# Batch 0's k in two halves of its heads on 96 partitions, its v let go by the second half's landing, and the last row tile in two column parts

## The chip, the cores and the metric

The kernel runs on one core of one Trainium2 chip. The metric is the device time of one execution in microseconds (us). Kernels are compared by executions on the same chip, one after the other. The granted clock is TensorE's clock as a share of full speed.

## The reference

Eight batches of attention with 8 heads, 576 positions and 64 columns a head. k and v are averaged over 8 neighbouring positions first, so that there are 72 pooled positions. Then a two-layer network with a GELU (tanh form) runs over all 4608 tokens.

```python
k_p = k.reshape(B, H, Sp, pool, D).mean(axis=3)          # B=8, H=8, S=576, D=64, pool=8, Sp=72
v_p = v.reshape(B, H, Sp, pool, D).mean(axis=3)
scores = scale * np.matmul(q, k_p.transpose(0, 1, 3, 2))
attn = softmax(scores)                                    # written out in the reference
x = (attn @ v_p).transpose(0, 2, 1, 3).reshape(B * S, H * D)     # 4608 x 512
h = x @ w_in                                              # 512 x 2048
out = gelu_tanh(h) @ w_out                                # 2048 x 512
```

## The kernel before

The network takes the tokens in 9 groups of 512. While TensorE runs the network for one group, the attention of a later batch is slipped in between. Batch 0 has nothing to hide behind: its attention is the head of the kernel, some 22 us. All inputs are fp32 in device memory. k's 576 rows of 2 KB (8 positions of 64 numbers) lie 4 to a partition on 128 partitions, and the last 64 rows in a fifth column block beside the end of v:

```python
KR = 4
kts = [consts.tile([128, KR + 1, 512], F32, name=f"kt{i}") for i in range(2)]

def load_k(b, engs):
    rows = k[b].rearrange("h (j l) d -> (h j) (l d)", l=8)
    main = rows[0:128 * KR].rearrange("(p r) c -> p r c", r=KR)
    n = KR // len(engs)
    for i, eng in enumerate(engs):
        eng.dma_start(out=kts[b % 2][:, i * n:(i + 1) * n], in_=main[:, i * n:(i + 1) * n])
    engs[0].dma_start(out=kts[b % 2][64:128, KR], in_=rows[128 * KR:])
    # ... and v's rows 64 to 71 of each head, into kts[b % 2][0:64, KR]

def load_v(b, engs):                      # v's rows 0 to 63: one half of the heads on 64 partitions each
    rows = v[b].rearrange("h (j l) d -> j h (l d)", l=8)
    for i in range(2):
        engs[i % len(engs)].dma_start(out=vts[b % 2][64 * i:64 * i + 64], in_=rows[0:64, 4 * i:4 * i + 4])

load_k(0, [nc.sync, nc.scalar])           # three queues: sync's, scalar's, GpSimd's
load_v(0, [nc.sync, nc.scalar])
load_q(0, 0, 1)                           # load_q, w_in, w_out: GpSimd's queue, cast to bf16 on the way
load_q(0, 1, 2)
load_w_in(0)
load_w_in(1)
load_k(1, [nc.gpsimd])
load_q(1)
load_v(1, [nc.gpsimd])
for i in range(4):                        # w_out in quarters
    ...
```

A batch's eight values are summed by three adds on VectorE (256, 128 and 64 columns wide), pooled k is turned by TensorE, the scores go through an exponential on ScalarE, and the products with pooled v are multiplied by an inverse of the sums (`inverse0`). `spin` puts matmuls on a zero tile into TensorE's waits; what that does for its clock is measured in warm and warm_full below (in warm_full the granted clock stays at full from 20.2 us on). The end of batch 0's attention:

```python
for f in v_steps(0):
    f()
inverse0(1, 0, 6)
spin(4, 4)
av0(0, 0, 4)                              # the first attention product
mult0(0, 0, 4)
den0(0, 2, 2)
inverse0(0, 2, 2)
av0(1, 0, 0)
# ... two more products with fillers between, then the clearing for batch 1, then the first layer
```

Each row tile of 128 tokens of the second layer is 16 matmuls of 512 columns, one copy out of PSUM and four stores.

The softmax here doesn't subtract the row's maximum and nothing guards it: scores larger than these inputs give would overflow.

## Time and profile before

| | |
|---|---|
| time | 309.19 us, median of 3 (308.62 to 309.35) |
| span of the profiled execution | 306.5 us, mean granted clock 0.999 |
| first attention product, first network layer | 17.18 and 22.08 us |
| landing of v of batch 0, of the last quarter of w_out | 14.45 and 43.99 us |
| start of the last copy out, from there to the end | 302.11 and 4.38 us |

The views are read thus. The page gives each engine's busy time and the chain of work that ended last. A line of the timeline is: start, length, engine, source line, operation, output and input tiles, and in brackets the idle time in front of it and what ended that. "Landing" is the moment the last of the 16 DMA engines reports a transfer done. The lines themselves are in the prediction below.

### The profile page before, as it was taken

What the parts mean: (1) busy time and instruction counts of PE and PEld (TensorE: products, weight loads), DVE (VectorE), ACT (ScalarE), POOL (GpSimd) and SP (SyncE); (2) the same over time, 40 slices, a digit from 0 to 9 for tenths busy, and PEclk for the clock granted to TensorE, in tenths of its full rate; (3) what the DMA queues carried; (4) which work ended last, traced back from release to release, by engine and by line L of the source; (5) the groups of instructions that cost most, each with busy time, mean ns of one, the idle gap of its engine ahead of it and who ended that gap; (6) DMA issues with size and microseconds to landing.
All of it is one profiled execution on the core that took longest, in us unless ns stands there. A gap on an engine that the chain in (4) does not pass through costs nothing.

```text
span 306.5 us, 4325 instructions
## 1 busy us (share of the span) xinstructions
PE 298.2 (97%) x1518; PEld 157.4 (51%) x1548; DVE 150.4 (49%) x334; ACT 219.0 (71%) x402; POOL 36.3 (12%) x69
## 2 busy tenths in 40 slices
PE   8999999999999999999999999999999999999994
PEld 3555555555555555555555555555555555445441
DVE  5868557573677057806681559245933630110021
ACT  1686679868987798779977998789868987206400
POOL 7103002305004000220014000400000000000000
PEclk9999999999999999999999999999999999999999
DMA  7999996987957952596159725662101210121022
GB/s 225 266 257 253 214 186 137 299 176 177 269 146 167 247 122 51 114 282 156 34 112 266 168 56 106 200 151 71 35 1 36 63 41 2 34 70 34 2 70 68
DMA packets 30359, 41.12 MB, mean 134 GB/s; under 512 B 18113, under 2 KB 18113, under 8 KB 29441
## 3 DMA queue, kind: packets, MB, share of 16 engines
q0 software_dynamic: 7856, 25.43, 34.9%
q1 hardware_dynamic: 21888, 14.09, 19.2%
q10 hardware_dynamic: 592, 1.31, 1.2%
q8 instruction: 12, 0.20, 0.3%
q14 instruction: 11, 0.08, 0.1%
HBM read 36.70 MB, written 9.44 MB: 151 GB/s over the span
## 4 chain that ended last, share of the span: by engine, by line
PE 83%; DMA 12%; POOL 1%; issue 1%; ACT 0%; DVE 0%; POOLq 0%
PE PS L345 38%; PE PS L336 36%; DMA kt<-in_k_dram 7%; DMA w_out_b<-in_moe_w_out_dram 5%; PE PS L239 4%; PE PS L261 4%; PE PS L174 1%; POOL w_in_b L105 0%; POOL qb L86 0%; POOL w_out_b L113 0%; DVE osb L350 0%; ACT e L247 0%; ACT ld L269 0%; ACT ld L268 0%; POOL identb masks.py:199 0%
## 5 line engine op out<-in xcount | busy, mean ns | idle before, releaser
L345 PE MATMUL PS<-w_out_b,gT 128*128 128x512 bf16 x560 | 134.2, 379 | 0.9
L336 PE MATMUL PS<-xT,w_in_b 128*128 128x512 bf16 x563 | 126.2, 379 | 0.6
L342 ACT ACTIVATE gT<-PS 128x512 bf16<-128x512 f32 x144 | 81.1, 604 | 47.5 <-PE PS L336 47.4
L336 PEld LDWEIGHTS <-w_in_b 128*128 128x128 bf16 x576 | 64.7, 113 | 57.2
L345 PEld LDWEIGHTS <-gT 128*128 128x128 bf16 x576 | 56.1, 97 | 56.7 <-issue 1.1
L350 DVE COPY osb<-PS 128x512 f32<-128x512 f32 x36 | 24.9, 691 | 98.3 <-PE PS L345 95.3
L279 DVE TENSOR_TENSOR xT<-PS,rc 64x288 bf16<-64x288 f32 x112 | 51.0, 455 | 31.6 <-ACT rc L271 29.3
L247 ACT ACTIVATE e<-PS 72x576 bf16<-72x576 f32 (+1 forms) x64 | 41.0, 646 | 9.1 <-PE PS L239 8.2
L239 PE MATMUL PS<-qT,kT 128*72 128x288 bf16 (+1 forms) x128 | 25.9, 286 | 0.9 <-ACT qT L214 0.6
L271 ACT ACTIVATE rc<-ld 128x288 f32<-128x288 f32 x56 | 24.8, 443 | 1.8
L314 ACT ACT_TABLE_LOAD x17 | 21.8, 1283 | 4.3 <-issue 4.1
L268 ACT ACTIVATE ld<-PS 64x288 f32<-64x288 f32 x56 | 22.8, 407 | 1.3
L269 ACT ACTIVATE ld<-PS 64x288 f32<-64x288 f32 x56 | 22.5, 402 | 1.3
L261 PE MATMUL PS<-e,vp 72*128 72x288 bf16 (+1 forms) x112 | 23.1, 286 | 0.0
L139 DVE TENSOR_TENSOR kt<-kt 128x1280 f32<-128x1280 f32 (+5 forms) x18 | 18.8, 1044 | 5.5 <-DMA kt<-in_v_dram 2.6
L239 PEld LDWEIGHTS <-kT 128*72 128x72 bf16 (+1 forms) x128 | 13.2, 105 | 15.2 <-DVE qT L216 1.2
L448 POOL COPY gate<-qT 1x2 bf16<-1x2 bf16 x6 | 1.0, 174 | 140.0 <-DMA qT<-qb 140.0
L139 DVE TENSOR_TENSOR vt<-vt 128x1024 f32<-128x1024 f32 (+1 forms) x16 | 15.3, 956 | 1.8 <-DMA vt<-in_v_dram 1.5
L184 DVE COPY kT<-PS 64x288 bf16<-64x288 bf16 (+2 forms) x48 | 13.0, 319 | 6.2 <-PE PS L174 6.1
L362 PE MATMUL PS<-idle 128*128 128x512 bf16 x39 | 11.9, 447 | 1.2 <-DVE idle L127 1.2
L261 PEld LDWEIGHTS <-vp 72*128 72x128 bf16 (+1 forms) x112 | 11.0, 98 | 3.8
L81 POOL DMA_DIRECT2D vt<-in_v_dram x14 | 9.0, 655 | 7.5 <-DMA w_in_b<-in_moe_w_in_dram 5.5
(47 smaller groups left out, 90.0 us busy)
## 6 DMA issues: line engine op xcount, KB each, us to landing
out_dram<-osb SPq DMA_DIRECT2D x142, 64.0 KB
kt<-in_k_dram POOLq DMA_DIRECT2D x7, 1024.0 KB, 6.2
vt<-in_v_dram POOLq DMA_DIRECT2D x14, 512.0 KB, 8.6
qb<-in_q_dram POOLq DMA_DIRECT2D x7, 576.0 KB, 11.6
w_in_b<-in_moe_w_in_dram POOLq DMA_DIRECT2D x2, 1024.0 KB, 16.7
w_out_b<-in_moe_w_out_dram POOLq DMA_DIRECT2D x4, 512.0 KB, 13.9
kt<-in_k_dram POOLq DMA_DIRECT2D x7, 128.0 KB, 5.9
kt<-in_v_dram POOLq DMA_DIRECT2D x14, 64.0 KB, 5.7
```

Of the source, the lines that this page charges most:

```text
L139: nc.vector.tensor_tensor(out=o, in0=a, in1=b, op=ALU.add)
L239: nc.tensor.matmul(out=PS[:n, bank + e, :CH].rearrange("j (t p) -> j t p", p=32), lhsT=kTs[b % 2][c][:, h, :n], rhs=qTs[b][:, h // 4, :, h ...
L247: nc.scalar.activation(out=e[:n], in_=PS[:n, bank:bank + 2, :CH], func=ACT.Exp, scale=1.0 / 64.0)
L261: nc.tensor.matmul(out=PS[:, bank + x, :CH], lhsT=window(vps[b % 2][:n], 2 * pr + x), rhs=e[:n, x, :], start=True, stop=True)
L268: nc.scalar.activation(out=ld[0:64], in_=PS[64:128, bank, :CH], func=ACT.Ln)
L269: nc.scalar.activation(out=ld[64:128], in_=PS[0:64, bank + 1, :CH], func=ACT.Ln)
L271: nc.scalar.activation(out=rc, in_=ld, func=ACT.Exp, scale=-1.0)
L279: nc.vector.tensor_tensor(out=xT[rows, pr, col:col + CH], in0=PS[rows, bank + x, :CH], in1=rc[rows], op=ALU.mult)
L336: nc.tensor.matmul(out=PS[:, h_bank(g, fo), c0:c1], lhsT=w_in_b[fo // 8][:, ko, q * 512 + j:(q + 1) * 512:4], rhs=xT[:, ko, r0 + c0:r0 + c ...
L342: nc.scalar.activation(out=gTs[g][:, fo, :], in_=PS[:, h_bank(g, fo), :], func=ACT.Gelu_apprx_tanh)
L345: nc.tensor.matmul(out=PS[:, o_bank(g, r), :], lhsT=gTs[g][:, fo, r * 128:(r + 1) * 128], rhs=w_out_b[:, fo, :], start=(fo == 0), stop=(fo ...
L350: nc.vector.tensor_copy(out=osb, in_=PS[:, o_bank(g, r), :])
```

## The change

Its intent: the first scores need only the lower half of the heads of k and the first half of q, so only these are fetched at first. Upper k follows in GpSimd's queue, and v, which is needed last, is held back until upper k has landed, so that it doesn't compete. A half of k has 288 rows, 3 to a partition on 96 partitions. Batch 1's v goes to sync's queue, the order after v is tightened, and the last row tile is cut into 384 and 128 columns so that its last copy is short.

```diff
-    KR = 4
+    KR = 3
-    kts = [consts.tile([128, KR + 1, 512], F32, name=f"kt{i}") for i in range(2)]
+    kts = [consts.tile([128, 2 * KR, 512], F32, name=f"kt{i}") for i in range(2)]
+    K0 = (0, 32)
+    def load_k(b, i, engs):
+        rows = k[b].rearrange("(i h) (j r l) d -> i (h j) (r l d)", i=2, r=KR, l=8)[i]
+        n = 4 * KH // len(engs)
+        for x, eng in enumerate(engs):
+            eng.dma_start(out=kts[b % 2][K0[i] + x * n:K0[i] + (x + 1) * n, KR * i:KR * i + KR],
+                          in_=rows[x * n:(x + 1) * n].rearrange("p (r c) -> p r c", r=KR))
 ...
-    load_k(0, [nc.sync, nc.scalar])
-    load_v(0, [nc.sync, nc.scalar])
+    load_k(0, 0, [nc.sync, nc.scalar])
     load_q(0, 0, 1)
+    load_k(0, 1, [nc.gpsimd])
+    load_v_last(0, nc.scalar)
     load_q(0, 1, 2)
 ...
     load_w_in(0)
+    for p in (slice(32, 64), slice(64, 128)):
+        nc.gpsimd.tensor_copy(out=vts[0][p, 0, 0:1], in_=kts[0][p, KR, 0:1])
+    load_v(0, [nc.sync])
     load_w_in(1)
 ...
-    load_v(1, [nc.gpsimd])
 ...
     inverse0(1, 0, 6)
-    spin(4, 4)
-    av0(0, 0, 4)
-    mult0(0, 0, 4)
+    spin(2, 4)
     den0(0, 2, 2)
     inverse0(0, 2, 2)
+    spin(2, 4)
+    av0(0, 0, 4)
+    mult0(0, 0, 4)
+    nc.vector.memset(vts[1][:, 0, 0:1], 0.0)
+    load_v(1, [nc.sync])
 ...
+    for t in kts:
+        nc.vector.memset(t[96:128, 0:KR], 0.0)
+    nc.vector.memset(kts[1][0:32, 2 * KR - 1], 0.0)
 ...
+    for c0, c1, bank in ((0, 384, o_bank(g, 3)), (384, DM, 4)):
+        for fo in range(FO):
+            p2_mm(g, 3, fo, bank, c0, c1)
+        store(g, 3, bank, c0, c1)
```

Cut: the transposes and copies of k by halves, v's last rows as two column blocks, fewer fillers, and the arguments that the column parts need. The two GpSimd copies are the hold: they read upper k and write into v's tile, so v's load can't be issued before upper k is in (in the profile after, upper k landed at 11.05 and sync issued v at 11.40).

More of the change, by code (lines that the diff above doesn't have):

```diff
@@ L63, with load_v_last @@
     vts = [consts.tile([128, 4, 512], F32, name=f"vt{i}") for i in range(2)]
-    kts = [consts.tile([128, KR + 1, 512], F32, name=f"kt{i}") for i in range(2)]
-    def load_k(b, engs):
-        rows = k[b].rearrange("h (j l) d -> (h j) (l d)", l=8)
-        main = rows[0:128 * KR].rearrange("(p r) c -> p r c", r=KR)
-        n = KR // len(engs)
-        for i, eng in enumerate(engs):
-            eng.dma_start(out=kts[b % 2][:, i * n:(i + 1) * n], in_=main[:, i * n:(i + 1) * n])
-        engs[0].dma_start(out=kts[b % 2][64:128, KR], in_=rows[128 * KR:])
+    kts = [consts.tile([128, 2 * KR, 512], F32, name=f"kt{i}") for i in range(2)]
[6 more added lines that the diff above has]
+                          in_=rows[x * n:(x + 1) * n].rearrange("p (r c) -> p r c", r=KR))
+    def load_v_last(b, eng):
         rows = v[b].rearrange("h (j l) d -> j h (l d)", l=8)
         for i in range(2):
-            engs[-1].dma_start(out=kts[b % 2][32 * i:32 * i + 32, KR], in_=rows[64:, 4 * i:4 * i + 4])
+            eng.dma_start(out=kts[b % 2][0:32, KR + i], in_=rows[64:, 4 * i:4 * i + 4])
     def load_v(b, engs):
@@ L107, with load_k_all @@
     load_w_in(0)
+    for p in (slice(32, 64), slice(64, 128)):
+        nc.gpsimd.tensor_copy(out=vts[0][p, 0, 0:1], in_=kts[0][p, KR, 0:1])
+    load_v(0, [nc.sync])
     load_w_in(1)
-    load_k(1, [nc.gpsimd])
+    def load_k_all(b):
+        for i in range(2):
+            load_k(b, i, [nc.gpsimd])
+        load_v_last(b, nc.gpsimd)
+    load_k_all(1)
     load_q(1)
-    load_v(1, [nc.gpsimd])
     for i in range(4):
@@ L119 @@
     kTs = [[consts.tile([128, H, 128], BF16, name=f"kT{i}{e}") for e in range(2)] for i in range(2)]
-    kps = [consts.tile([128, KR + 2, D], BF16, name=f"kp{i}") for i in range(2)]
+    kps = [consts.tile([128, 2 * KR + 1, D], BF16, name=f"kp{i}") for i in range(2)]
     vps = [consts.tile([128, H, 2, D], BF16, name=f"vp{i}") for i in range(2)]
@@ L127 @@
     nc.vector.memset(idle, 0.0)
+    nc.vector.memset(kts[0][0:32, 2 * KR - 1], 0.0)
     nc.vector.memset(kTs[0][0], 0.0)
@@ L139, in add, with k_steps @@
         nc.vector.tensor_tensor(out=o, in0=a, in1=b, op=ALU.add)
-    def k_steps(b, c=slice(0, KR + 1)):
-        t = kts[b % 2]
+    def k_steps(b, i0=0, i1=2):
+        c = slice(i0 * KR, i1 * KR)
+        n = K0[i1 - 1] + 4 * KH
+        t = kts[b % 2][0:n]
         return [lambda: add(t[:, c, 0:256], t[:, c, 0:256], t[:, c, 256:512]),
                 lambda: add(t[:, c, 0:128], t[:, c, 0:128], t[:, c, 128:256]),
-                lambda: add(kps[b % 2][:, c], t[:, c, 0:64], t[:, c, 64:128])]
+                lambda: add(kps[b % 2][0:n, c], t[:, c, 0:64], t[:, c, 64:128])]
     def v_moves(b):
@@ L152, in v_moves @@
             nc.sync.dma_start(out=vps[b % 2][64 - 64 * i:72 - 64 * i, 4 * i:4 * i + 4, 0],
-                              in_=kps[b % 2][32 * i:32 * i + 32, KR])
+                              in_=kps[b % 2][0:32, KR + i])
     def v_steps(b):
@@ L168, in half_bank, with trans_k_mm @@
         return PS[:, bank, :].bitcast(BF16)
-    def trans_k_mm(b, bank, r0=0, r1=KR + 1, n=128):
-        tp = half_bank(bank)[:, 0:(KR + 1) * 128].rearrange("p (r c) -> p r c", c=128)
+    def trans_k_mm(b, i, bank):
+        tp = half_bank(bank)[:, 0:2 * KR * 128].rearrange("p (r c) -> p r c", c=128)
         kf = kps[b % 2].rearrange("p r d -> p (r d)")
-        for r in range(r0, r1):
-            nc.tensor.transpose(out=tp[:n, r, :], in_=kf[:, r * D:r * D + n], identity=identb)
-    def trans_k_copy(b, e, bank, lower=True, upper=True):
-        tp = half_bank(bank)[0:D, 0:(KR + 1) * 128].rearrange("p (r c) -> p r c", c=128)
-        o = kTs[b % 2][e][e * 64:(e + 1) * 64]
-        copy = nc.vector.tensor_copy
-        def heads(h0, h1, c0, j0, j1):
-            copy(out=o[:, h0:h1, c0:c0 + (j1 - j0) * KR].rearrange("p h (j r) -> p h j r", r=KR),
-                 in_=tp[:, 0:KR, h0 * KH:h1 * KH].rearrange("p r (h j) -> p h j r", j=KH)[:, :, j0:j1])
-        if lower:
-            heads(0, 4, 0, 0, KH)
-        if upper:
-            heads(4, H - 1, 64, 0, 16)
-            heads(4, H - 1, 0, 16, KH)
-            copy(out=o[:, H - 1, 64:72].rearrange("p (j r) -> p j r", r=KR),
-                 in_=tp[:, 0:KR, (H - 1) * KH:128].rearrange("p r j -> p j r"))
-            copy(out=o[:, H - 1, 72:128], in_=tp[:, KR, 64:120])
-            copy(out=o[:, H - 1, 0:8], in_=tp[:, KR, 120:128])
@@ new lines, in trans_k_mm, with trans_k_copy, part @@
+        n, m = (128, 128) if b else (K0[i] + 4 * KH, D)
+        for r in range(i * KR, i * KR + KR):
+            nc.tensor.transpose(out=tp[0:m, r, 0:n], in_=kf[0:n, r * D:r * D + m], identity=identb[0:n, 0:n])
+    def trans_k_copy(b, e, i, bank):
+        tp = half_bank(bank)[0:D, 0:2 * KR * 128].rearrange("p (r c) -> p r c", c=128)
+        tp = tp[:, i * KR:i * KR + KR, K0[i]:K0[i] + 4 * KH].rearrange("p r (h j) -> p h j r", j=KH)
+        o = kTs[b % 2][e][e * 64:(e + 1) * 64, 4 * i:4 * i + 4]
+        def part(c0, j0, j1, r0=0, r1=KR):
+            n = r1 - r0
+            nc.vector.tensor_copy(out=o[:, :, c0:c0 + (j1 - j0) * n].rearrange("p h (j r) -> p h j r", r=n),
+                                  in_=tp[:, :, j0:j1, r0:r1])
+        if i == 0:
+            part(0, 0, KH)
+        else:
+            part(64, 0, 21)
+            part(127, 21, 22, 0, 1)
+            part(0, 21, 22, 1, 3)
+            part(2, 22, KH)
@@ L197, in trans_k @@
     def trans_k(b, bank):
-        trans_k_mm(b, bank)
+        for i in range(2):
+            trans_k_mm(b, i, bank)
         for e in range(2):
-            trans_k_copy(b, e, bank)
+            for i in range(2):
+                trans_k_copy(b, e, i, bank)
     def trans_q_mm(b, i, t0, n, bank):
@@ L342, in gelu, with p2_mm, store @@
         nc.scalar.activation(out=gTs[g][:, fo, :], in_=PS[:, h_bank(g, fo), :], func=ACT.Gelu_apprx_tanh)
-    def p2_mm(g, r, fo):
-        nc.tensor.matmul(out=PS[:, o_bank(g, r), :], lhsT=gTs[g][:, fo, r * 128:(r + 1) * 128], rhs=w_out_b[:, fo, :],
-                         start=(fo == 0), stop=(fo == FO - 1))
-    def store(g, r):
-        osb = opool.tile([128, DM], F32, name="osb")
-        nc.vector.tensor_copy(out=osb, in_=PS[:, o_bank(g, r), :])
+    def p2_mm(g, r, fo, bank, c0=0, c1=DM):
+        nc.tensor.matmul(out=PS[:, bank, c0:c1], lhsT=gTs[g][:, fo, r * 128:(r + 1) * 128],
+                         rhs=w_out_b[:, fo, c0:c1], start=(fo == 0), stop=(fo == FO - 1))
+    osbs = {}
+    def store(g, r, bank, c0=0, c1=DM):
+        if (g, r) not in osbs:
+            osbs[g, r] = opool.tile([128, DM], F32, name="osb")
+        osb = osbs[g, r]
+        nc.vector.tensor_copy(out=osb[:, c0:c1], in_=PS[:, bank, c0:c1])
         for n in range(4):
-            b, c = divmod(g * GROUP + r * 128 + n * 32, S)
+            b, col = divmod(g * GROUP + r * 128 + n * 32, S)
             rows = out[b * S:(b + 1) * S].rearrange("(p t e) d -> e t p d", t=TP, e=2)
-            eng = nc.scalar if (g, r) == (NG - 1, 3) and n % 2 else nc.sync
-            eng.dma_start(out=rows[c // CH, c % CH // 32], in_=osb[n * 32:(n + 1) * 32, :])
+            eng = nc.scalar if c1 - c0 < DM and n % 2 else nc.sync
+            eng.dma_start(out=rows[col // CH, col % CH // 32, :, c0:c1], in_=osb[n * 32:(n + 1) * 32, c0:c1])
     def spin(n, bank):
@@ L364 @@
     act_set(EXP_SET)
-    spin(22, 1)
-    for f in k_steps(0, slice(0, KR)):
+    spin(13, 1)
+    for f in k_steps(0, 0, 1):
         f()
@@ L371, in scores @@
         expo(0, c, pr, bank)
-    trans_k_mm(0, 4, 0, KR, D)
-    trans_k_copy(0, 0, 4, upper=False)
     trans_q(0, *QG[0], 5, nc.scalar)
-    trans_q(0, *QG[1], 6, nc.vector)
-    trans_k_copy(0, 1, 4, upper=False)
+    trans_q(0, *QG[1], 6, nc.scalar)
+    spin(3, 4)
+    trans_k_mm(0, 0, 4)
+    trans_k_copy(0, 0, 0, 4)
+    trans_k_copy(0, 1, 0, 4)
     scores(0, 0, 2)
@@ L380 @@
     spin(2, 7)
-    for f in k_steps(0, slice(KR, KR + 1)):
+    for f in k_steps(0, 1, 2):
         f()
     scores(1, 0, 2)
-    trans_k_mm(0, 4, KR, KR + 1, D)
-    trans_k_copy(0, 0, 4, lower=False)
+    trans_k_mm(0, 1, 4)
+    trans_k_copy(0, 0, 1, 4)
     for h in range(H):
@@ L389 @@
         nc.tensor.matmul(out=PS[64 - 64 * i:72 - 64 * i, 7, h * D:(h + 1) * D],
-                         lhsT=identb[0:64, 32 * i + h % 4:32 * i + 32:4], rhs=kps[0][0:64, KR],
+                         lhsT=identb[0:32, h % 4:32:4], rhs=kps[0][0:32, KR + i],
                          start=True, stop=True)
@@ L400 @@
     trans_q(0, *QG[3], 6, nc.vector)
-    trans_k_copy(0, 1, 4, lower=False)
+    trans_k_copy(0, 1, 1, 4)
     spin(3, 7)
@@ L410 @@
     inverse0(1, 0, 6)
-    spin(4, 4)
+    spin(2, 4)
+    den0(0, 2, 2)
+    inverse0(0, 2, 2)
+    spin(2, 4)
     av0(0, 0, 4)
     mult0(0, 0, 4)
-    den0(0, 2, 2)
-    inverse0(0, 2, 2)
+    nc.vector.memset(vts[1][:, 0, 0:1], 0.0)
+    load_v(1, [nc.sync])
+    den0(1, 2, 6)
+    inverse0(1, 2, 6)
     av0(1, 0, 0)
     mult0(1, 0, 0)
-    spin(3, 6)
-    den0(1, 2, 6)
-    inverse0(1, 2, 6)
-    spin(3, 4)
     av0(0, 2, 4)
     mult0(0, 2, 4)
-    spin(3, 0)
+    spin(2, 0)
     av0(1, 2, 0)
@@ L427 @@
     for t in kps:
-        nc.vector.memset(t[:, KR + 1], 0.0)
+        nc.vector.memset(t[:, 2 * KR], 0.0)
+    for t in kts:
+        nc.vector.memset(t[96:128, 0:KR], 0.0)
+    nc.vector.memset(kts[1][0:32, 2 * KR - 1], 0.0)
     nc.vector.memset(kTs[1][0], 0.0)
@@ L448, in load_next @@
             nc.gpsimd.tensor_copy(out=gate, in_=qTs[g + 2][0:1, 1, TP - 1, 0:2])
-            load_k(g + 2, [nc.gpsimd])
+            load_k_all(g + 2)
             load_v(g + 2, [nc.gpsimd])
@@ L512 @@
                     at(min(pos[i] + 9, 62 if i < len(ORDER) else 65), mult, *a)
-        seq = [(r, fo) for r in range(4) for fo in range(FO)]
+        seq = [(r, fo) for r in range(4 if g + 1 < NG else 3) for fo in range(FO)]
         if g == 0:
@@ L519 @@
                 f(*a)
-            p2_mm(g, r, fo)
+            p2_mm(g, r, fo, o_bank(g, r))
             if fo == FO - 1:
-                store(g, r)
+                store(g, r, o_bank(g, r))
         for m in sorted(todo):
```

## The prediction

> **What bounds the kernel now.** First the page, by engine and by chain.
>
> ```profile
> PE 298.2 (97%) x1518; PEld 157.4 (51%) x1548; DVE 150.4 (49%) x334; ACT 219.0 (71%) x402; POOL 36.3 (12%) x69
> ...
> PE 83%; DMA 12%; POOL 1%; issue 1%; ACT 0%; DVE 0%; POOLq 0%
> ```
>
> TensorE is busy for 97% of the span, but 40 of its matmuls are fillers on a zero tile; the first 22 us are the pooled attention of batch 0 and give little. The chain has 12% of DMA in it. In order of time it starts so:
>
> ```profile
> 4.55 21.57 DMA kt<-in_k_dram
> 26.12 0.28 issue
> 26.40 0.86 POOL w_out_b L113 x2
> 27.46 16.53 DMA w_out_b<-in_moe_w_out_dram
> 44.03 0.81 PE PS L345 x3
> ```
>
> So until 44 us transfers set the pace: the last quarter of w_out lands at 43.99 and TensorE takes it at 44.03. Next the table by stretches (columns: stretch, its length, busy us and count of PE, PEld, DVE, ACT, POOL, then granted clock, DMA share, GB/s): the DMA engines are never free.
>
> ```profile
> 8.00:12.00 4.00, 3.39 (x34) 2.06 (x33) 2.87 (x10) 2.40 (x4) 1.39 (x2) 1.00 1.07 293
> 12.00:14.00 2.00, 1.95 (x17) 1.12 (x15) 1.94 (x8) 1.84 (x4) 0.02 (x1) 1.00 1.13 248
> 14.00:22.00 8.00, 7.66 (x50) 4.65 (x50) 5.71 (x12) 6.96 (x12) 0.62 (x1) 1.00 1.12 229
> ```
>
> Then the timeline of the head, for the hand-offs (start, length, engine, line, what, and in brackets the idle time before it and what ended it). Batch 0's scores start at 9.85, v's adds at 14.72 without an idle time before them, the first attention product waits for pooled v, and the first real layer starts at 22.08.
>
> ```profile
> 9.85 0.65 PE L239 MATMUL PS<-qT,kT 128*72 128x288 bf16 x4 [0.56 <-ACT qT L214]
> ...
> 14.72 1.95 DVE L139 TENSOR_TENSOR vt<-vt 128x1024 f32<-128x1024 f32 x2
> ...
> 17.18 0.66 PE L304 MATMUL PS<-e,vz 72*128 72x288 bf16 x4 [0.17 <-DVE vz L139]
> ...
> 22.08 11.17 PE L336 MATMUL PS<-xT,w_in_b 128*128 128x512 bf16 x50
> ...
> 40.94 1.68 PE L345 MATMUL PS<-w_out_b,gT 128*128 128x512 bf16 x6
> ...
> 42.94 1.90 PE L345 MATMUL PS<-w_out_b,gT 128*128 128x512 bf16 x7
> ```
>
> From the trace's landings: k's main part 5.78, q's first half 8.30, second 11.07, v's halves 12.72 and 14.45, w_in 17.22 and 23.03, next k 26.12, w_out's quarters 36.60, 39.09, 41.55, 43.99.
>
> Back to back a matmul of 512 columns takes 0.216, and the last of a group shows 0.163 more: six should take 1.46 and seven 1.68. The groups at 40.94 and 42.94, where the third and last quarters are first read, take 1.68 and 1.90, so TensorE waited 0.22 for each, 0.4 in all. **A head shortened by x saves x only if w_out comes x sooner as well; one lengthened by x costs x less 0.4.**
>
> [...]from 12 to 13 us 64 packets of v (scalar's queue) stand beside 68 of w_in (GpSimd's); from 10 to 11 us three queues moved 54, 54 and 56.[...] with two queues v has two shares of three, with one it has one of two.[...] The trace: 1225 ns at 1024 and 691 at 512[...].[...] The trace: fillers 0.427 us apart until 5.8 us, 0.216 after[...].
>
> **The change, part by part.**
>
> *Lower k.* 590 KB rather than 1 MB are needed first. The sync queue's packets began at 1.81; 256 of 4 KB took till 5.3. A 6 KB packet should take between the 159 ns of 4 KB and the 299 ns of 8 KB, say 230; 96 of them on 16 engines are 1.4 us, so landing near 4.3. Adds of 768, 384 and 192[...]: 0.96+0.56+0.36=1.9, pooled at 6.3 against 8.21. But q's first half comes first on TensorE now; GpSimd's packets began only at 4.75, need 128x191 ns/16=1.5 us alone, and the last engine landed 1.2 after the bulk: 7.4. Nine transposes 0.65, three fillers 0.65, three transposes, a copy of 0.45: scores at 9.35. **Gain 0.5 us there.**
>
> *Upper k.* Its adds run on 128 partitions x768 (1.9 us) where 0.98 us stood, copies are 4 per parity in place of 5. VectorE, busy from 9.8, is done with both at about 15.7, where it was at 14.68. So the gain of the scores is lost again by the time v's adds could start.
>
> *v of batch 0.* This I take as the deciding step. It is issued when upper k has landed. Upper k follows q's first half in GpSimd's queue: 96x230 ns/16=1.4 us, so in by 7.8, landing 8.7 with the same straggler. Two small GpSimd copies, then sync issues near 9.1; first packet 1.1 us later, as at the start: 10.2. It is now on sync's queue alone, beside w_in in GpSimd's queue: 64 packets per us, 512 packets, 8.0 us. Landing near 18.7 (was 14.45). Adds and first pooled v 2.46 us (14.72 to 17.18): the attention product starts at 21.15, 4.0 later. From there the rest is shorter, as the second pair's inverse is put ahead of it and fillers are fewer: product, multiply, product into the freed bank, filler, last product, 3.5 us where 4.9 stood. **First layer at 24.65, 2.6 late.** w_in's first half (17 us) is in time.
>
> *More clearing.* VectorE zeroes two pieces of 32x1536 and one of 32x512 in fp32 before batch 1's k. 512 words took 0.485, so 1.33+1.33+0.49=3.2 us more, and k's adds are 3.3 for 2.77. VectorE idled 2.64 us before 33.85, so 1 us comes through, in part absorbed by copies: batch 1's transposes of k wait 0.3, its first pooled v 0.15. **Cost 0.5.**
>
> *v of batch 1* goes from GpSimd's queue (q's landing 30.28 to v's 34.89, 4.6 us) to sync's (512 packets at 92 ns/16=2.9 us). w_out should land at some 42 to 43, not 43.99. It takes the 0.4 us of waits away, no more, as TensorE is late itself.
>
> *Later batches.* Six transposes for five, at 0.055 us, and adds that VectorE (49%) hides: six batches, **0.3 us.**
>
> *Last row tile.* 16 matmuls of 384 and 16 of 128 columns for 16 of 512: 16x(0.162+0.057) to 16x0.216, 0.05 more. The last copy is 128 columns, 0.29 by the 0.69 of 512, so 0.4 sooner.
>
> ```profile
> 302.11 0.69 DVE L350 COPY osb<-PS 128x512 f32<-128x512 f32 x1 [2.76 <-PE PS L345]
> 302.84 0.85 ACTq L356 DMA_DIRECT2D out_dram<-osb  x2
> ```
>
> But each queue has now four issues of 0.43 there, two of them still running when the copy ends, so the last issue is only 0.2 sooner, and 16 KB pieces land perhaps 0.15 sooner than 64 KB ones. **Gain 0.3.**
>
> Sum: +2.6+0.5-0.4+0.3-0.3=+2.7 us on 309.2: 311.9.
>
> **Rivals.** (a) *v is in time*, if its queue gets more than an equal share or upper k lands by 7. Then VectorE's 15.7 sets it: product at 18.2, first layer at 21.7, 0.4 early; with +0.5 for the clearing, -0.4 for the waits, +0.3 and -0.3 as above this is 308.8; at best, with q in at 6.5, 306.8. The change's fillers speak for it: they are cut from 40 to 27, as if the author had seen shorter waits. The measured shares speak against it. (b) *TensorE goes to half clock* in the 4 us that it would wait for v[...]. (c) *Everything is hidden by w_out*: if w_out still landed at 43.99, an early head would give nothing and only the tail's 0.3 be left: 308.9. The 1.7 us that batch 1's v saves speak against it.
>
> **Range and chances.** Six tenths on the sum (311.9), four tenths on (a) or (c) (about 308.2): 310.4. The range goes from the best of (a) to past the sum, 307.0 to 312.8. Two per cent is 6.2 us, over twice any sum here: faster 0.01, slower 0.03.
>
> **What would show it.** Right: lower k lands before 5, scores start between 9 and 9.6, v's adds begin after 17.5 with an idle time put down to v's DMA, the first layer starts after 23.5, w_out's matmuls wait for nothing, TensorE's end to the span's end is 4.1 rather than 4.4. Wrong, if v's adds start by 16 or the first layer before 22; or if a wait for w_out is still there. The step I trust least is v's share of the DMA engines.

The two times that stand after the count of packets, 1225 and 691 ns, are those of the fp32 adds of 1024 and 512 columns a partition in the profile before. The 0.96, 0.56 and 0.36 us for adds of 768, 384 and 192 columns are an estimate: they lie on the straight line through these two (the profile after has 1.54 us for the first two and 0.35 for the third).

## The result, and the profile after

The changed kernel takes 318.99 us (median of 4, 318.17 to 319.71) for 309.03 (median of 4) of the kernel before. The ratio is 1.0322, with a 95% interval of 1.0288 to 1.0356: slower by over 2%. (The two profiled executions below differ by a little more, 11.4 us, as the changed kernel's was its slowest, 319.71 us, and the other's one of its fastest, 308.29 us.) Ratios here are the mean time of one kernel's fast runs over that of the other's in the same rounds, so they are not quite the ratio of the medians.

The page, by engine, and its chain in summary:

```profile
PE 301.9 (95%) x1530; PEld 160.2 (50%) x1559; DVE 156.6 (49%) x323; ACT 219.4 (69%) x403; POOL 35.8 (11%) x70
...
PE 82%; DMA 7%; DVE 4%; ACT 3%; issue 1%; POOL 0%; SPq 0%; DVEq 0%; POOLq 0%; ACTq 0%
```

TensorE is busy 3.7 us longer while it has 13 fillers fewer, and the span is 11.4 longer: it waits, and it works more slowly. The chain in order of time (start, length, what) says on what. It has two transfers of batch 0 in a row at the start, and no w_out any more:

```profile
1.94 9.11 DMA kt<-in_k_dram
12.21 12.63 DMA vt<-in_v_dram
29.49 1.92 PE PS L324 x8
43.49 1.62 DVE kt L154
```

The same stretches as in the prediction (stretch, length, busy us and count of PE, PEld, DVE, ACT, POOL, then granted clock, DMA share, GB/s), and one more:

```profile
8.00:12.00 4.00, 2.96 (x23) 1.69 (x23) 1.25 (x3) 2.16 (x4) 0.68 (x3) 1.00 1.09 216
12.00:14.00 2.00, 0.48 (x5) 0.29 (x3) 1.52 (x3) 0.81 (x2) 2.00 (x4) 0.85 1.12 213
14.00:22.00 8.00, 7.72 (x47) 4.90 (x46) 2.97 (x12) 4.59 (x8) 2.50 (x5) 0.61 1.10 244
22.00:34.00 12.00, 6.98 (x27) 3.53 (x26) 5.60 (x9) 4.95 (x7) 1.76 (x3) 0.72 1.07 235
```

From 8 to 14 us fewer bytes arrive than before (216 and 213 GB/s for 293 and 248), though the DMA engines are as busy (share 1.09 and 1.12 for 1.07 and 1.13). The granted clock, 1.00 in the rows of before, is 0.61 and 0.72. The hand-offs in the timeline, one engine after the other:

```profile
10.55 0.68 PE L259 MATMUL PS<-qT,kT 128*72 128x288 bf16 x4 [0.54 <-DVE kT L204]
...
11.19 0.42 POOL L114 COPY vt<-kt 32x1 f32<-32x1 f32 x2 [6.88 <-DMA kt<-in_k_dram]
...
11.40 1.41 SPq L84 DMA_DIRECT2D vt<-in_v_dram  x2
...
24.93 1.23 DVE L154 TENSOR_TENSOR vt<-vt 128x1024 f32<-128x1024 f32 x1 [6.68 <-DMA vt<-in_v_dram]
...
27.39 1.14 PE L324 MATMUL PS<-e,vz 72*128 72x288 bf16 x4 [5.02 <-DVE vz L154]
...
33.13 3.13 PE L356 MATMUL PS<-xT,w_in_b 128*128 128x512 bf16 x11
```

Upper k lands at 11.05, the copies end the hold, sync issues v's halves, its first packet moves at 13.6, and the halves land at 20.50 and 24.83. VectorE idles 6.68 us for them. Note also the length of the first product: 1.14 us for four matmuls that took 0.66 before. Later in the kernel two lines matter: the wait for batch 1's pooled k, and the tail.

```profile
46.75 0.51 PE L193 MATMUL PS<-identb,kp 128*128 128x128 bf16 x6 [0.49 <-DVE kp L154]
...
313.89 1.79 ACTq L380 DMA_DIRECT2D out_dram<-osb  x4
314.20 0.29 DVE L374 COPY osb<-PS 128x128 f32<-128x128 f32 x1 [0.34 <-PE PS L365]
```

So the account of the two profiled executions is complete:

| piece | before | after | difference | forecast |
|---|---|---|---|---|
| VectorE done with batch 0's k, free for v | 14.69 | 18.24 | +3.55 | +1.0 |
| its wait for v | 0.03 | 6.68 | +6.65 | +3.0 |
| v's adds to the first product | 2.46 | 2.46 | 0 | 0 |
| first product to the first layer | 4.90 | 5.74 | +0.84 | -1.4 |
| first layer to the last copy | 280.03 | 281.07 | +1.04 | +0.4 |
| last copy to the end | 4.38 | 3.74 | -0.64 | -0.3 |
| span | 306.49 | 317.93 | +11.44 | +2.7 |

(The gap of 0.03 us ahead of v's adds before is the pause between two instructions.)

### The profile page after: what moved, and what is told of

Its sections match the earlier page's. It is cut to its first block, busy times and chain, and to the rows that moved or that the text cites. A ratio compares the mean times of both kernels' runs of the same rounds, so it can differ in the third digit from the quotient of the medians.

```text
span 317.9 us, 4350 instructions
## 1 busy us (share of the span) xinstructions
PE 301.9 (95%) x1530; PEld 160.2 (50%) x1559; DVE 156.6 (49%) x323; ACT 219.4 (69%) x403; POOL 35.8 (11%) x70
## 4 chain that ended last, share of the span: by engine, by line
PE 82%; DMA 7%; DVE 4%; ACT 3%; issue 1%; POOL 0%; SPq 0%; DVEq 0%; POOLq 0%; ACTq 0%
PE PS L365 37%; PE PS L356 34%; PE PS L259 4%; PE PS L281 4%; DMA vt<-in_v_dram 4%; DMA kt<-in_k_dram 3%; PE PS L324 1%; PE PS L193 1%; DVE kt L457 1%; DVE kt L154 1%; ACT ld L289 1%; ACT ld L288 1%; ACT e L267 1%; ACT gT L362 1%; DVE vt L154 1%
## 5 line engine op out<-in xcount | busy, mean ns | idle before, releaser
L365 PE MATMUL PS<-w_out_b,gT 128*128 128x512 bf16 (+2 forms) x578 | 134.0, 373 | 0.7
L365 PEld LDWEIGHTS <-gT 128*128 128x128 bf16 x592 | 57.1, 98 | 55.6 <-issue 0.4
L374 DVE COPY osb<-PS 128x512 f32<-128x512 f32 (+2 forms) x37 | 25.1, 677 | 101.0 <-PE PS L365 97.9
L259 PE MATMUL PS<-qT,kT 128*72 128x288 bf16 (+1 forms) x128 | 26.6, 295 | 0.7 <-DVE kT L204 0.5
L154 DVE TENSOR_TENSOR kt<-kt 128x768 f32<-128x768 f32 (+4 forms) x18 | 22.0, 1220 | 2.8 <-DMA kt<-in_k_dram 1.7
L204 DVE COPY kT<-PS 64x252 bf16<-64x252 bf16 (+4 forms) x80 | 16.3, 264 | 7.1 <-PE PS L193 7.0
L386 PE MATMUL PS<-idle 128*128 128x512 bf16 x26 | 10.5, 538 | 1.4 <-DVE idle L140 1.2
L324 PE MATMUL PS<-e,vz 72*128 72x288 bf16 (+1 forms) x16 | 4.4, 443 | 5.0 <-DVE vz L154 5.0
```

The lines of the kernel that those rows point to most:

```text
L154: nc.vector.tensor_tensor(out=o, in0=a, in1=b, op=ALU.add)
L259: nc.tensor.matmul(out=PS[:n, bank + e, :CH].rearrange("j (t p) -> j t p", p=32), lhsT=kTs[b % 2][c][:, h, :n], rhs=qTs[b][:, h // 4, :, h ...
L365: nc.tensor.matmul(out=PS[:, bank, c0:c1], lhsT=gTs[g][:, fo, r * 128:(r + 1) * 128], rhs=w_out_b[:, fo, c0:c1], start=(fo == 0), stop=(fo ...
L374: nc.vector.tensor_copy(out=osb[:, c0:c1], in_=PS[:, bank, c0:c1])
```

## The experiments

All ran against the kernel before in the same rounds. The times inside a kernel are those of its profiled execution. The runs of one kernel lie within 2.4 us of one another or less with k as before, and within up to 4.7 us with k by halves.

### Is it the hold on v? v_at_once and before_gated

One takes the hold out of the changed kernel, the other puts it into the kernel before.

```diff
 v_at_once (from the changed kernel)
-    for p in (slice(32, 64), slice(64, 128)):
-        nc.gpsimd.tensor_copy(out=vts[0][p, 0, 0:1], in_=kts[0][p, KR, 0:1])
     load_v(0, [nc.sync])
 before_gated (from the kernel before)
-    load_v(0, [nc.sync, nc.scalar])
 ...
     load_w_in(0)
+    for p in (slice(0, 64), slice(64, 128)):
+        nc.gpsimd.tensor_copy(out=vts[0][p, 0, 0:1], in_=kts[0][64:128, KR, 0:1])
+    load_v(0, [nc.sync])
```

> The changed kernel without the two GpSimd copies that hold batch 0's v back; v goes out on sync's queue right behind lower k. Theory (the hold-back is what costs): v's adds start near 14 to 18 rather than at 24.93, the first layer near 24 to 26 rather than at 33.13, time 309.5 to 312. Rival (TensorE's half clock after idling is the main cost, whatever v does): over 315. Rival (upper k, now sharing the DMA engines with v, arrives so late that the gain is lost): adds of upper k after 14, time over 314.

> The kernel before with one part of the change alone: batch 0's v is held back until the last piece of k has landed (7.6 us), and is issued on sync's queue alone. Theory: issue near 8, landing near 18 to 20 (was 14.45), the first layer 4 to 6 us later than 22.08, time 313 to 316. Rival (k by halves with its slow 96-partition transfers is what costs): under 311.

Measured: v_at_once 313.41 us, ratio 1.0135 (1.0104 to 1.0167); before_gated 316.47 us, ratio 1.0232 (1.0209 to 1.0255). Both are a little slower than I expected. The timeline of v_at_once, VectorE's adds of v and the first product and first layer:

```profile
19.52 1.95 DVE L152 TENSOR_TENSOR vt<-vt 128x1024 f32<-128x1024 f32 x2
...
22.16 0.66 PE L322 MATMUL PS<-e,vz 72*128 72x288 bf16 x4
...
25.64 0.59 PE L354 MATMUL PS<-xT,w_in_b 128*128 128x512 bf16 x2
```

and of before_gated:

```profile
20.66 1.95 DVE L141 TENSOR_TENSOR vt<-vt 128x1024 f32<-128x1024 f32 x2 [5.58 <-DMA vt<-in_v_dram]
...
23.11 1.14 PE L306 MATMUL PS<-e,vz 72*128 72x288 bf16 x4 [5.71 <-DVE vz L141]
...
29.89 2.32 PE L338 MATMUL PS<-xT,w_in_b 128*128 128x512 bf16 x9
```

With k as before, the hold (with v on sync's queue alone, which this edit also brings) makes a wait of 5.58 us, and in v_at_once, where only the hold is taken out, no bracket for v is left. In before_gated v is issued at 7.40, but its first packet starts at 11.34 only, and the last half lands at 20.56; TensorE's clock is at half from 20.18 to 27.0. Four kernels in a square:

| ratio to before | v at once | v held |
|---|---|---|
| k whole | 1 | 1.0232 |
| k by halves | 1.0135 | 1.0322 |

The hold costs 1.9 points with k by halves, where v is on one queue in both kernels; with k whole it costs 2.3% together with the step from two queues to one, which was not run apart. The rest, 1.35%, belongs to k by halves, to v on one queue, and to the smaller parts that came with it: without the hold v isn't waited for, yet its adds start at 19.52 instead of 14.72. VectorE gets upper k's rows that much later (they land at 13.49 there, at 11.05 in the changed kernel, where v is fetched after them), and TensorE's clock is at half from 10.30 to 17.13.

### Is it that v is on one queue? gated_two_queues

The held load's second half goes to scalar's queue, which can issue it after its third exponential (the argument that picks the half is cut from the diff).

```diff
-    load_v(0, [nc.sync])
+    load_v(0, [nc.sync], [0])
 ...
     scores(1, 0, 2)
+    load_v(0, [nc.scalar], [1])
     trans_k_mm(0, 1, 4)
```

> The changed kernel with v still held back, but its second half issued on scalar's queue behind the third exponential. Theory (v's share of the DMA engines[...] set its pace): v lands near 21 to 22 rather than 24.83, time 315.5 to 316.5. Rival (the landing is set by the moment of release alone): no change, 318.5 to 319.5.

Measured: 316.15 us, ratio 1.0236 (1.0175 to 1.0297). v's halves land at 20.55 and 21.63 instead of 20.50 and 24.83. VectorE still waits:

```profile
21.73 1.95 DVE L154 TENSOR_TENSOR vt<-vt 128x1024 f32<-128x1024 f32 x2 [5.50 <-DMA vt<-in_v_dram]
```

So v is in 3.2 us sooner when it has two queues beside w_in's; one queue's share was the step that I had trusted least. But the two halves, of 64 partitions each, are then also written at the same time; which of the two helps, this run can't tell. Against the kernel before, where v lands at 14.45, 7 us remain: the larger part is the late start (first packet at 13.94). (VectorE's wait shrinks by 1.2 us only, as VectorE was done with k 2.0 us sooner in this execution; upper k had landed 0.7 us sooner.)

### Is it TensorE's clock? warm and warm_full

More fillers ahead of the first product, 20 and 34 for 2:

```diff
     inverse0(0, 2, 2)
-    spin(2, 4)
+    spin(20, 4)        # warm; spin(34, 4) in warm_full
     av0(0, 0, 4)
```

> The changed kernel with 18 more filler matmuls in the wait for v, so that TensorE is at full clock when v is there. From the first attention product to the first layer 5.74 us were measured where 3.5 were forecast. Theory (half clock is the difference): 3.6 us, time 316.8 to 317.4. Rival (the ring of two buffers for the inverses, which stops ScalarE from 23.7 to 29.5, is the difference): no change, 318.5 to 319.5.

> The changed kernel with 34 fillers in place of 2 ahead of the first attention product, so that TensorE has work until v is there (20 of them ended 2.8 us too early and its clock fell all the same). Theory: v still lands near 24, the granted clock stays at 1.0 from 15 to 30, product to first layer takes 3.5 us rather than 5.74, first layer at 30.0 to 30.5, ratio 1.024 to 1.026. Rival: ScalarE's inverses and not TensorE's clock stretch this piece: it stays over 4.7 and the time does not move (ratio 1.031).

Measured: warm 318.61 us, ratio 1.031 (1.0263 to 1.0356); warm_full 318.4 us, ratio 1.029 (1.0261 to 1.032). In warm the fillers ended too early, TensorE idled 2.81 us, and the clock fell again: the run was inconclusive. Its stretches from 20 to 30 us (the third number from the right is the granted clock):

```profile
20.00:25.00 5.00, 3.22 (x15) 1.27 (x13) 1.39 (x2) 0.61 (x1) 0.39 (x1) 1.00 1.08 272
25.00:30.00 5.00, 3.90 (x17) 2.46 (x18) 2.94 (x7) 1.39 (x3) 0.84 (x3) 0.66 1.07 227
```

In warm_full the clock stays full from 20.2 us on, and the piece from the first product to the first layer takes what the prediction gave it:

```profile
28.94 0.66 PE L324 MATMUL PS<-e,vz 72*128 72x288 bf16 x4
...
32.42 0.81 PE L356 MATMUL PS<-xT,w_in_b 128*128 128x512 bf16 x3
```

That is 3.48 us for 5.74. So the half clock is worth 2.26 us of this piece, and ScalarE's inverses are not its bound. A gain in time isn't resolved (the intervals of warm_full and the changed kernel overlap); the fillers overran pooled v, whose first half was there at 27.0, by 1.9 us. My expectation of a full clock from 15 us was wrong: in this run too it was 0.50 from 15 to 20, before the added fillers.

### Can the same order be had without a wait? v_in_order, and two repairs

v goes into GpSimd's queue between q's second half and w_in. In these traces the transfers of GpSimd's queue land in the order of their issue (in the changed kernel q's first half at 8.40, upper k 11.05, q's second half 12.03, w_in 18.41 and 25.94), so v should come after k and q, and nothing has to wait for a landing and be issued afterwards.

```diff
+    load_v(0, [nc.gpsimd])
     load_w_in(0)
-    for p in (slice(32, 64), slice(64, 128)):
-        nc.gpsimd.tensor_copy(out=vts[0][p, 0, 0:1], in_=kts[0][p, KR, 0:1])
-    load_v(0, [nc.sync])
```

> The changed kernel with v of batch 0 in GpSimd's queue behind q's second half and ahead of w_in, with no wait: the same order of arrival, kept by one queue instead of by a landing. Theory: the wait on the landing (issue round trip, then sharing with w_in) was the loss. v lands at 16.5 to 18, VectorE's work on upper k ends at 18.2 and is the bound, v's adds start at 18.3 to 18.8 with little or no idle, product at 20.8, first layer at 24.3; ratio 1.008 (1.005 to 1.012). Rival: v's halves on 64 partitions each are slow wherever they stand (213 GB/s seen for batch 1's): v lands after 19.5 and the ratio is as without the wait, 1.0135, or above.

Measured: 313.31 us (311.92 to 316.57), ratio 1.0171 (1.0121 to 1.0221). The head did better than I expected, and then the time was lost elsewhere:

```profile
17.16 1.95 DVE L152 TENSOR_TENSOR vt<-vt 128x1024 f32<-128x1024 f32 x2
...
23.28 2.97 PE L354 MATMUL PS<-xT,w_in_b 128*128 128x512 bf16 x12
...
37.59 0.45 PE L222 MATMUL PS<-identb,qb 128*128 128x128 bf16 x5 [2.92 <-DMA qb<-in_q_dram]
```

v's halves land at 13.76 and 16.37, after q's second half at 11.43, and the first layer starts at 23.28 rather than 33.13. But batch 1's q now lands at 37.5, and TensorE waits 2.92 us for it. I blamed batch 1's v, which the change had put on sync's queue from 21 us on. The next kernel puts it back behind q, and does the clearing earlier as well.

```diff
 k_halves_best (from v_in_order)
     load_q(1)
+    load_v(1, [nc.gpsimd])
 ...                      # two clearings move up; that of kts[1][96:128] stays where it was
+    nc.vector.memset(kts[0][96:128, 0:KR], 0.0)
+    nc.vector.memset(kts[1][0:32, 2 * KR - 1], 0.0)
     trans_k_copy(0, 0, 0, 4)
 ...
-    nc.vector.memset(vts[1][:, 0, 0:1], 0.0)
-    load_v(1, [nc.sync])
```

> What k by halves can give without the two costs around it: v of batch 0 in GpSimd's queue behind q's second half, no wait (as in the run v_in_order, whose first layer started at 23.28), v of batch 1 back in GpSimd's queue behind q (v_in_order waited 2.92 us for that q), and two of the three clearings in VectorE's idle time at 7 to 9.6. Theory: v's adds at 17.2 to 17.5, first layer at 23.3 to 23.6, no wait for q of batch 1, first layer to last copy 280.0 to 280.5, time 309.8 to 310.6, ratio 1.003 to 1.005. So k by halves costs the head some 1.3 us against the kernel before even so. Rival: q's wait comes from the total of transfers and not from v of batch 1: then over 282 from first layer to last copy and ratio over 1.010.

Measured: 316.04 us (314.16 to 318.86), ratio 1.0223 (1.0172 to 1.0274). A miss, twice over: in the profile (of the slowest of its four runs) the first layer starts at 26.69, not at the 23.3 to 23.6 expected, with the clock at half from 9.38 to 19.62; and q's wait shrank to 0.59 us, but w_out's took its place.

```profile
46.49 2.35 PE L364 MATMUL PS<-w_out_b,gT 128*128 128x512 bf16 x6 [3.72 <-DMA w_out_b<-in_moe_w_out_dram]
```

Its landings show stragglers. Of the 16 DMA engines, 12 finished upper k by 9.24 us and four between 11.76 and 12.19. In every later transfer of GpSimd's queue, too, four engines came in after the other twelve, by 0.8 to 2.5 us, up to w_out's last quarter (12 engines by 50.63 us, the last four between 51.50 and 53.89). (The trace doesn't say whether they are the same four.) A transfer counts as landed with its slowest engine. In the changed kernel's profile three engines came in after the other 13 in every transfer of that queue from q's first half to batch 1's q, the first of the three 0.6 to 1.8 us after the 13th. In the profile of the kernel before, the 16 landings of k's main parts lie within 0.75 us of one another. What makes the stragglers is the subject of the next runs; that they differ from run to run fits the wide spread of all kernels with k by halves.

### What is the cost of 96 partitions? k_two_packets, k_6kb_on_128, k_4kb_on_96

I had put a 6 KB packet at 230 ns. In the changed kernel, lower k's took 392 and 378 ns in the mean on the two queues, with hardly anything else in flight, and upper k's and batch 1's k's together 367 (upper k's alone 321). Either long packets are slow, or the 96 partitions are. The first run cuts upper k of batch 0 in the changed kernel into 4 and 2 KB a partition. The other two change the kernel before: one has 6 and 2 KB packets on 128 partitions, the other 4 KB packets on 96 partitions with the rest of k zeroed, which computes something else. (Its output still passed the comparison, so the tolerance doesn't see it.)

```diff
 k_two_packets (from the changed kernel)
+            for r0, r1 in ((0, 2), (2, 3)) if (b, i) == (0, 1) else ((0, 3),):
+                eng.dma_start(out=..., KR * i + r0:KR * i + r1], in_=...[:, r0:r1])
 k_6kb_on_128 (from the kernel before)
+            c = (slice(0, 3), slice(3, 4))[i]          # for batch 0 only
+            eng.dma_start(out=kts[b % 2][:, c], in_=main[:, c])
 k_4kb_on_96 (from the kernel before)
+            m = 96 if b == 0 else 128
+            eng.dma_start(out=kts[b % 2][:m, i * n:(i + 1) * n], in_=main[:m, i * n:(i + 1) * n])
+    nc.vector.memset(kts[0][96:128, 0:KR], 0.0)
```

> The changed kernel with batch 0's upper k in two transfers, rows 0 to 1 (4 KB a partition) and row 2 (2 KB), in place of one of 6 KB. It tells apart why the 6 KB packets took 366 ns in the mean rather than the 230 I forecast. Packet-size theory: long packets are slow; 4 KB at 159 ns and 2 KB at 92 ns, both as seen in the kernel before, are 251 ns a partition, so upper k lands 0.7 to 1 us sooner, at 10.0 to 10.4 rather than 11.05, and v's issue with it. Partition theory[...]: nothing gained, upper k lands at 10.8 to 11.4. The time is 318 either way, ratio 1.028 to 1.033.

> The kernel before with batch 0's k, on all 128 partitions as it was, cut into 6 KB and 2 KB a partition in place of 4 and 4. Partition theory: 6 KB packets take 234 to 300 ns (159 by 6/4 is 239). Length theory: they take 360 or more, as in the changed kernel.

> The kernel before with only partitions 0 to 95 of batch 0's k loaded and the rest zeroed: the result is wrong on purpose, the packets stay 4 KB. Partition theory: 4 KB packets take 240 to 260 ns in the mean (384 by 4/6 is 256) where they took 169 and 202 on 128 partitions, so that three quarters of the bytes take as long as all did. Length theory: 160 to 200 ns, and the load is done a quarter sooner.

Measured: k_two_packets 317.26 us, ratio 1.0251 (1.0211 to 1.0291), upper k landing at 10.55, between the two forecasts, in an execution with few stragglers; this run alone does not decide. The other two were single looks at 310.1 and 309.14 us (state unknown, granted clock 0.997 and 1.0). Their packets tell the two apart:

| batch 0's k, main part | packet | partitions | mean ns of a packet, by queue | landing |
|---|---|---|---|---|
| before | 4 KB | 128 | 202 and 169 | 5.62 and 5.78 |
| k_6kb_on_128 | 6 KB (other queue 2 KB) | 128 | 289 (median 234) | 5.69 and 5.90 |
| k_4kb_on_96 | 4 KB | 96 | 258 and 232 | 6.42 and 6.77 |
| changed kernel, lower k | 6 KB | 96 (48 from each queue) | 392 and 378 | 4.95 and 5.54 |

With 96 partitions three quarters of the bytes came 1.0 us **later** than all of them on 128. The adds in k_4kb_on_96 start so (before: 5.80):

```profile
6.79 1.23 DVE L141 TENSOR_TENSOR kt<-kt 128x1024 f32<-128x1024 f32 x1 [1.06 <-DMA kt<-in_k_dram]
```

And five of its 16 DMA engines are stragglers, 0.5 to 0.8 us behind the other eleven, where k of the kernel before shows none. So it is the partitions that make the packets slow: by the KB, 4 KB packets take 51 and 42 ns on 128 partitions and 65 and 58 on 96; 6 KB packets take 48 on 128, and 65 and 63 for lower k. In these two, length adds nothing beyond its bytes. (That lower k comes as two transfers of 48 partitions was not tested apart.) The stragglers are less clear: in k_6kb_on_128 seven of 16 engines landed q's two parts 0.5 to 0.8 us after the slowest of the other nine, with all loads of k on 128 partitions. What in the hardware makes either is not seen in these traces.

### Is it the clearing? clear_early and v_at_once_clear

The three clearings of unused k rows (3.2 us of VectorE) are moved to where VectorE idles: before v's adds in the changed kernel, and before the first copies of k in v_at_once.

```diff
 clear_early (from the changed kernel)
+    for t in kts:
+        nc.vector.memset(t[96:128, 0:KR], 0.0)
+    nc.vector.memset(kts[1][0:32, 2 * KR - 1], 0.0)
     for f in v_steps(0):
         f()
 ...                      # and taken away after the last product
```

> The changed kernel with the clearing of the unused k rows (3.2 us of VectorE) moved from after the last product to before v's adds, where VectorE idles 6.7 us for v. Theory: batch 1's pooled k is then in time, so TensorE's waits of 0.49 for it and 0.2 for its v go: first layer to last copy 280.4 to 280.6 rather than 281.07, time 318.4 for 319.0, ratio 1.029 to 1.031. Rival: k of batch 1 itself lands too late (28.3 and 30.6) and nothing is gained: 281.0 to 281.1.

> The run v_at_once (no hold on v, ratio 1.0135) with the clearing of the unused k rows moved into VectorE's idle 5.3 us before the first copies. Theory: first layer still at 25.6, first layer to last copy 280.0 to 280.3 rather than 281.14 (the clearing cost 1.04 in the run clear_early), time 312.3 to 312.6, ratio 1.010 to 1.011: that is what k by halves costs by itself. Rival: w_out or batch 1's q takes the place of the wait for k, ratio 1.013 or more.

Measured: clear_early 317.8 us, ratio 1.0273 (1.024 to 1.0306); v_at_once_clear 312.19 us, ratio 1.0101 (1.0075 to 1.0126). In both, 280.03 us lie between the first layer and the last copy, for 281.07 and 281.14. The transposes of batch 1's k no longer wait in clear_early:

```profile
45.81 0.50 PE L193 MATMUL PS<-identb,kp 128*128 128x128 bf16 x6
```

The late clearing cost 1.04 us in the profile, twice my 0.5; as a time, with intervals that overlap, it isn't resolved. And 1.0101 is what k by halves costs with the hold and the late clearing out of the way, with v on one queue, tail and tightened order included. (In v_at_once_clear's profile, of its slowest run, upper k landed at 14.17 and the first layer started at 27.84, not at the 25.6 expected.)

### What are the other parts worth? tail_on_before, before_reordered, reordered_v1_late

The first has the tail alone. The second has the tail, the tightened order after v and batch 1's v on sync's queue, with k and v of batch 0 as before. The third lets batch 1's v go after the last product instead of after the first.

```diff
 before_reordered (from the kernel before, with the tail's two column parts)
-    load_v(1, [nc.gpsimd])
     inverse0(1, 0, 6)
-    spin(4, 4)
-    av0(0, 0, 4)
-    mult0(0, 0, 4)
+    spin(2, 4)
     den0(0, 2, 2)
     inverse0(0, 2, 2)
+    spin(2, 4)
+    av0(0, 0, 4)
+    mult0(0, 0, 4)
+    nc.vector.memset(vts[1][:, 0, 0:1], 0.0)
+    load_v(1, [nc.sync])
 ...                      # fewer fillers, the last inverse sooner, and the tail's lines
 reordered_v1_late (from before_reordered)
     mult0(1, 2, 0)
+    nc.vector.memset(vts[1][:, 0, 0:1], 0.0)      # these two from above to here
+    load_v(1, [nc.sync])
```

> The kernel before with one part of the change alone: the last row tile in column parts of 384 and 128. Theory: in the changed kernel the tail is worth 0.64 us from the start of the last copy (4.38 to 3.74) plus what the copy starts sooner or later; here the same: the head stays at 22.1 for the first layer, last copy to end 3.74, time 308.3 to 308.6 for 309.0, ratio 0.998. Rival: the two parts' extra issues cost as much as the shorter copy gains: ratio 1.000.

> The kernel before with the parts of the change that do not touch batch 0's k and v: the tail, the second pair's inverse ahead of the first product with fewer fillers, and batch 1's v on sync's queue in the head. Theory: product to first layer takes 3.5 us in place of 4.90, first layer at 20.7 rather than 22.08; w_out lands 1 to 2 us sooner as batch 1's v no longer stands in front of it, so that most of this comes through; with the tail 307.0 to 307.6, ratio 0.994. Rival: w_out still lands at 44, then the early head is given back in waits for w_out and only the tail is left: ratio 0.998.

> The run before_reordered (307.31 us) with one change: batch 1's v let go after the last product's multiply, some 2.5 us later. In before_reordered TensorE waited 0.56 us for q of batch 1 at 32.65, beside which v was being fetched since 20. Theory: with v later, k and q of batch 1 land 0.5 us sooner and that wait goes; 306.8, ratio 0.993. Rival: v then stands beside w_out and w_out's wait takes its place: 307.3 or above, ratio 0.995 to 0.997.

Measured: tail_on_before 308.63 us, ratio 0.9993 (0.9974 to 1.0011); before_reordered 307.31 us, ratio 0.9947 (0.993 to 0.9964); reordered_v1_late 307.94 us, ratio 0.9955 (0.9928 to 0.9981). The tail's last piece shrank from 4.38 to 3.85 us in the profile, but as a time this isn't resolved. The reordering is: first product at 17.23, first layer at 20.70, 3.47 us.

```profile
17.23 0.66 PE L303 MATMUL PS<-e,vz 72*128 72x288 bf16 x4
...
20.70 3.62 PE L335 MATMUL PS<-xT,w_in_b 128*128 128x512 bf16 x15
...
32.65 0.45 PE L203 MATMUL PS<-identb,qb 128*128 128x128 bf16 x5 [0.56 <-DMA qb<-in_q_dram]
```

Of the 1.4 us won, 0.56 went to a wait for batch 1's q. Letting v go later removed that wait and put another in its place, as the rival there said, though for v and not for w_out:

```profile
40.59 0.42 PE L260 MATMUL PS<-e,vp 72*128 72x288 bf16 x2 [0.98 <-DVE vp L138]
```

before_reordered is the version that beats both kernels: the one before by 0.5%, the changed one, by the medians, by 3.7%.

## Why the prediction was wrong

The direction of the sum was right: v late, the first layer late. "Upper k landed, then v" was named as the deciding step. But the sum was +2.7 us where the profiles show +11.44, and the four tenths of weight on the rivals (a) and (c) pulled 311.9 down to 310.4. Point by point:

- **Lower k and the scores** (forecast: landing 4.3, scores 9.35, a gain of 0.5). Landing 4.95 and 5.54, q's first half 8.40 for 7.4, scores 10.55: a loss of 0.7. One wrong term is the 230 ns of a 6 KB packet, which came from 128 partitions (where k_6kb_on_128 has a median of 234) and was carried over to 96. The packets took 378 to 392, and lower k was pooled at 7.49 for 6.3. But the scores waited for q: 13 engines had brought its first half by 6.96, three only between 8.20 and 8.40.
- **Upper k, VectorE done at 15.7.** It was 18.24. Upper k landed at 11.05 instead of 8.7: the same packet term, and three DMA engines 1.1 us or more behind the other 13. Then TensorE's half clock from 13.41 us stretched the steps between VectorE's (nine transposes of q took 1.17 us, for 0.68 at 8.44). This is 2.5 us of the miss.
- **v's issue, share and landing** (9.1, 8.0 us, 18.7). Issued at 11.40 because upper k was late. The first packet came 2.2 us after that rather than 1.1, which I had taken from the start of the program (DMA share 0.12 in the first 2 us of the kernel before, 1.12 from 12 to 14 us of the changed one). In the seven runs that hold v, from the issue of its first load to its first packet, it was 2.1 to 4.0 us. From the first packet to the landing passed 11.2 us rather than 8.5: its packets took 118 ns in the mean, 96 in before_gated, where it was 9.2 us. So v landed 6.1 us late, 2.3 from the issue, 1.1 from the start, 2.7 from the transfer. The wait of 6.68 us where 3.0 were forecast is the largest single miss, 3.7 us. v_at_once and before_gated show that it comes with the hold, gated_two_queues that one queue (and one half of the partitions at a time) is the smaller part.
- **Product to first layer in 3.5 us.** 5.74 with the clock at half, 3.48 in warm_full and v_at_once: the order of the work was right, and rival (b), half clock in the wait for v, happened and cost 2.26. I had counted on fillers in the wait; 5.02 us without one were left, and the clock was at half from 27.06 to 33.89. It had also been at half from 13.41 to 20.23, which the prediction didn't have: it fell in a wait of 1.52 us for upper k. In v_in_order it fell at 12.61, after a wait of 0.89 us, in warm after one of 2.81 us; yet a wait of 1.63 us, 6.81 to 8.44 in the changed kernel, left it up. What decides it is not shown.
- **Clearing 0.5.** 1.04, by clear_early.
- **No wait for w_out.** Right, but only because the head was so late: the last quarter was to land at 42 to 43 and lands at 47.09, later than before; the second layer starts at 49.32.
- **Extra transposes 0.3, w_out's waits -0.4.** Together nothing: with the clearing moved, 280.03 us, exactly as before. Not tested apart.
- **Tail -0.3.** -0.64 and -0.53 in the two profiles; not resolved in time. That smaller pieces land sooner (0.15) was a guess; from the start of the last issue to the end of the span the profiles have 3.24 us before, with 64 KB pieces, and 2.67 after, with 16 KB.
- **Rivals (a) and (c)** fell: v's adds begin after 17.5, as the prediction's own test had it.
- **Small slips in its figures.** The terms of (a) add up to 308.9, not 308.8; 8 KB packets take 309 ns in the median, not 299; and the 306.8 of (a) at best lies outside the range.

The step of the working that failed is thus not the order of events but the terms of "v of batch 0": a landing at 18.7 was forecast and 24.83 measured. Mis-sized were how long 96 partitions take to be written, how late a transfer starts that waits for another's landing while all engines are busy, and how long it then takes; and the wait for a late transfer went with a half clock here as well (2.26 us). All point the same way, so they add, and my range, built around one forecast and two cheaper rivals, gave rival (b) no weight and had no room on that side. What stays open: why the transfer of v itself was slower than in before_gated, which DMA engines are the slow ones, and why their number differs from run to run.

## What to carry to other kernels

Fewer bytes on fewer partitions need not come sooner (in k_4kb_on_96 three quarters of the bytes landed at 6.77 for 5.78, in a single look): price a load by packets measured at the same number of partitions, and look at the landing of its slowest DMA engine. To have one transfer come after another, put both in one queue in that order, as v_in_order did (first layer at 23.28 for 33.13, though the time lost elsewhere left it at 1.0171, no better than v_at_once); the hold on a landing added here 0.35 us to the issue, 2.2 from there to the first packet, and a share near the half: from 16 to 22 us 353 packets of v started beside 390 of GpSimd's queue. And an idle TensorE cost twice here, once as the wait (5.02 us) and again as the half clock after it (2.26).
